# Second group's seven-product MLPs: input sums and parts spread over the first steps, weight splits at the head of a step, first two pairs interleaved

## The chip, the core and the metric

The kernel runs on one core of a Trainium2 chip. The metric is the time of one execution on the device in microseconds (us), the median of three runs. TensorE (PE) multiplies matrices, VectorE (DVE), ScalarE (ACT) and GpSimd (POOL) work element by element, and SyncE (SP) issues most of the transfers. Each engine takes its instructions strictly in the order in which they were written.

## What is computed

An attention with mixing across heads, and behind it two MLPs on the same 1792 tokens (4 batches of 448), all in float32:

```python
def _moe_ref(x, w_in, w_out):       # x (1792, 768), w_in (768, 2048), w_out (2048, 768)
    h = x @ w_in
    r = np.maximum(h, 0.0)
    g = r * r
    return g @ w_out

def _moe2_ref(x, w_in, w_out):
    h = x @ w_in
    g = h * np.clip(h + 3.0, 0.0, 6.0) / 6.0
    return g @ w_out

def reference(...):
    attn = _attn_ref(q, k, v, w_pre, w_post)        # per batch, 12 heads, 448 x 448
    x = attn.transpose(0, 2, 1, 3).reshape(B * S, H * D)
    return _moe2_ref(_moe_ref(x, ...), ...)
```

## The kernel before

The four batches are worked in two groups of two. For each group the attention runs first, then both MLPs. The order is written by hand: what stands in the program is what each engine's queue holds. The change touches only the MLPs of the second group (`SevenMlps`) and the last slots of the attention before them. Group 2 has no further attention to hide behind, so its MLPs stand alone at the end of the program.

Numbers are carried as a high part and a low part (`wh`, `wl`; `xh`, `xl`; `gh`, `gl`): ACT writes the high part as a rounded copy, DVE or POOL then writes the low part, source minus high part. A product is three matmuls, high by high, low by high, high by low.

The first matrix product of each MLP is done with seven block products in place of eight. A *pair* `j` is two blocks of 128 hidden features (`2j`, `2j+1`) for the two batches (`e` = 0, 1); the 768 input features are two halves of 3 blocks. Each product `P1` to `P7` multiplies one combination of weight blocks by one of inputs:

```python
FACTORS = {
    "P1": ("A11", "B11"), "P2": ("A12", "B21"), "P3": ("S4", "B22"), "P4": ("A22", "T4"),
    "P5": ("S1", "T1"), "P6": ("S2", "T2"), "P7": ("S3", "T3"),
}
```

A, B are blocks of weights and inputs; S1 = A21+A22, S2 = S1-A11, S3 = A11-A21, S4 = A12-S2 and T1 = B12-B11, T2 = B22-T1 (the tile `t2`), T3 = B22-B12, T4 = B21-T2 are sums made on DVE. A *step* is one product of one pair: 9 matmuls of 448 columns (3 blocks by 3). P1 and P2 share a PSUM bank (`bm`), P6, P5 and P3 another (`bo`), P7 and P4 a third (`bx`): a later product is added on top of an earlier one, so the earlier sum has to be read out of the bank before the later product may start. P1 is read by a copy on ACT (`s`), P6, P5, P7, P3 and P4 by an addition on DVE (`u`, `s`); the activation makes `g`, and `gh`/`gl` are its parts.

An MLP runs in two parts of 8 hidden blocks: 28 steps of products (4 pairs), then 8 steps of the second matrix product (`project`, 36 matmuls each, two halves of outputs `dg`). So group 2 has four stages of 28 steps, each followed by 8 projection steps. `steps` is sorted by `7 * j + SLOTS[name]`; in the first part of each MLP, P2 and P1 of the first two pairs have slots of their own.

`run` walks over the steps. At step `t` before the change:

- deferred work of earlier steps comes first (`todo[t]`, filled by `later`: the second half of the activation, then `last`, which makes `gh` on ACT and `gl` on POOL);
- then the weights for three steps ahead are split (`make`, `AHEAD = 4` buffers): `wh` on ACT, `wl` on DVE for A12, S3, S1 and on POOL for the others. With A11's split DVE also makes the three sums of the pair (L783 to L785); S4 (L790) follows when A12 and S2 have both been split;
- then come the 9 matmuls and the reading of their bank.

The inputs of the first MLP are prepared in the last slots of the attention (`opening`, `between`): the parts of B11 and B21 and the sums T1. At the head of `run`, `last_inputs` then does the rest at once: for each of 3 columns T3, `t2`, the part of T2 and T4, and then the parts of T1, T3, B22 and T4. For the second MLP, `finish` of the last projection step of the first one calls the same `last_inputs` (T1 has its parts by then).

## Time and profile before

| | us |
|---|---|
| three runs | 1478.33, 1482.08, 1482.3 |
| median | 1482.08 |
| profiled execution, its own time | 1478.12 |
| its span, first to last instruction | 1476.3 |

| engine | busy us | share of the span |
|---|---|---|
| PE | 1386.4 | 94% |
| DVE | 905.4 | 61% |
| ACT | 701.4 | 48% |
| POOL | 641.1 | 43% |

The mean granted TensorE clock is 0.985 of full speed. Group 2's MLPs run from 972.1 us to the end. A busy PE is no sign of full pace, since matmuls are pipelined and one that runs at half clock is busy too: the pace of a stage is its time divided by its matmuls. The waits that count are those that PE has, and each must be followed back through the queues of the other engines.

### The profile page before, as it was taken

Reading aid. Unit: us, or ns where it says so; the run is one execution under the profiler, and the core shown is the slowest. Engines: PE = TensorE matmul, PEld = TensorE weight load, DVE = VectorE, ACT = ScalarE, POOL = GpSimd, SP = SyncE. Lnnn points to the kernel's source line nnn. Section 1 sums busy time; section 2 is a strip of 40 time slices with the busy share of each in tenths; the row PEclk is TensorE's granted clock in tenths of the full one; section 3 lists DMA queues with packets and bytes.
Section 4 is the critical chain, followed back from the end, with each engine's and each line's share of the span. In section 5 each row is a group of like instructions: output and inputs, shape, how many; then the busy total and the mean of one; then the engine's idle time right before and its main releaser. Section 6 shows DMA issues by size and latency. Waiting matters only on the chain. (4 is left out here: it accounts for less than half of the span.)

```text
span 1476.3 us, 23273 instructions
## 1 busy us (share of the span) xinstructions
PE 1386.4 (94%) x8368; PEld 1231.7 (83%) x8368; DVE 905.4 (61%) x1662; ACT 701.4 (48%) x1428; POOL 641.1 (43%) x677
## 2 busy tenths in 40 slices
PE   8889998999999999999989999969999996999999
PEld 4778887999999999998978788857898785789788
DVE  4887566877665788775466866777307437721731
ACT  4776665555332455444366666633233324533530
POOL 1767675333200133200046767745525634552551
PEclk9999999999999999999999999979999998999999
DMA  5444533555555555666444454401211210121121
GB/s 145 117 141 113 147 102 105 177 160 161 163 158 162 159 160 161 177 199 197 164 119 130 115 142 116 133 13 44 75 44 54 65 54 21 55 65 44 43 69 70
DMA packets 72215, 167.56 MB, mean 113 GB/s; under 512 B 9125, under 2 KB 47525, under 8 KB 72101
## 3 DMA queue, kind: packets, MB, share of 16 engines
q1 hardware_dynamic: 68645, 160.59, 37.3%
q10 hardware_dynamic: 3456, 5.51, 1.0%
q8 instruction: 65, 1.06, 0.3%
q14 instruction: 49, 0.40, 0.1%
HBM read 96.86 MB, written 30.67 MB: 86 GB/s over the span
## 5 line engine op out<-in xcount | busy, mean ns | idle before, releaser
L226 POOL TENSOR_TENSOR tl<-t,th 120x448 fp32r<-120x448 f32 x165 | 193.3, 1171 | 31.8 <-ACT th L224 30.5
L281 PEld LDWEIGHTS ps_o<-w2s,p 120*112 120x112 f32 (+1 forms) x1440 | 173.2, 178 | 23.9 <-POOL w2s L270 14.2
L281 PE MATMUL ps_o<-w2s,p 120*112 120x120 f32 (+1 forms) x1440 | 180.1, 268 | 8.6 <-POOL w2s L270 8.6
L571 POOL TENSOR_TENSOR gl<-g,gh 128x448 fp32r<-128x448 f32 x40 | 52.3, 1309 | 210.7 <-ACT gh L570 164.1
L250 ACT ACTIVATE p<-ps_m,mx 120x448 f32<-120x448 f32 x180 | 113.2, 629 | 64.3 <-PE ps_o L281 29.1
L296 DVE COPY a<-ps_o 112x480 f32<-112x480 f32 (+1 forms) x176 | 114.3, 650 | 29.2 <-PE ps_o L281 28.0
L270 POOL TENSOR_SCALAR w2s<-w2f,rz 120x120 f32<-120x120 f32 x180 | 69.3, 385 | 131.0 <-DVE rz L262 119.1
L224 ACT ACTIVATE th<-t 120x448 fp32r<-120x448 f32 x180 | 102.6, 570 | 47.7 <-POOL tl L226 19.2
L242 DVE TENSOR_REDUCE mx<-ps_m 120x1 f32<-120x448 f32 x180 | 109.2, 606 | 19.5 <-PE ps_m L235 19.5
L535 ACT ACTIVATE wh<-arena 128x384 fp32r<-128x384 f32 x128 | 62.0, 516 | 115.4 <-PE bs L591 104.8
L536 DVE TENSOR_TENSOR wl<-arena,wh 128x384 fp32r<-128x384 f32 x128 | 69.1, 568 | 77.0 <-ACT wh L535 75.8
L767 POOL TENSOR_TENSOR wl<-arena,wh 128x384 fp32r<-128x384 f32 x64 | 64.9, 1032 | 102.4 <-ACT wh L766 102.4
L965 PE MATMUL ps_a<-gh,wl 128*128 128x448 f32 x272 | 99.6, 366 | 1.6 <-POOL wl L767 1.4
L181 POOL TENSOR_TENSOR ql<-qr,qh 128x440 fp32r<-128x440 f32 (+1 forms) x42 | 48.6, 1156 | 117.8 <-ACT qh L180 105.6
L965 PE MATMUL ps_a<-gh,wh 128*128 128x448 f32 x272 | 99.3, 365 | 0.0
L591 PE MATMUL ps_a<-gh,wh 128*128 128x448 f32 x256 | 93.7, 366 | 0.0
L591 PE MATMUL ps_a<-gh,wl 128*128 128x448 f32 x256 | 93.4, 365 | 0.0
L233 PE MATMUL ps_m<-th,w1h 120*120 120x448 f32 x180 | 81.6, 453 | 8.0 <-ACT p L250 6.6
L308 PE MATMUL ps_x<-a,v 112*64 112x110 f32 (+1 forms) x1536 | 84.6, 264 | 4.5 <-DVE xr L316 3.4
L766 ACT ACTIVATE wh<-arena 128x384 fp32r<-128x384 f32 x64 | 32.8, 519 | 116.7 <-PE bs L965 73.3
L308 PEld LDWEIGHTS ps_x<-a,v 112*64 112x64 f32 x1536 | 74.6, 138 | 10.3 <-DVE xr L316 3.8
L235 PE MATMUL ps_m<-tl,w1h 120*120 120x448 f32 x180 | 68.9, 383 | 12.6 <-POOL tl L226 12.6
(200 smaller groups left out, 3862.7 us busy)
## 6 DMA issues: line engine op xcount, KB each, us to landing
arena<-in_dram SPq DMA_DIRECT2D x64, 768.0 KB
t<-s SPq DMA_DIRECT2D x176, 210.0 KB
keep<-arena SPq DMA_DIRECT2D x64, 384.0 KB
arena<-keep SPq DMA_DIRECT2D x64, 384.0 KB
qr<-in_dram SPq DMA_DIRECT2D x60, 110.0 KB
v<-in_dram SPq DMA_DIRECT2D x12, 448.0 KB
outT_dram<-ot ACTq DMA_DIRECT2D x24, 224.0 KB
kr<-in_dram SPq DMA_DIRECT2D x18, 224.0 KB
```

Of the source, the lines that this page charges most:

```text
L224: nc.scalar.activation(th[:rows], tt[:rows], AF.Copy)
L226: eng.tensor_tensor(out=tl[:rows], in0=tt[:rows], in1=f(th[:rows]), op=ALU.subtract)
L233: nc.tensor.matmul(m[:rows, :S], lhsT=w1h[:rows, :rows], rhs=th[:rows], start=True, stop=False)
L242: nc.vector.reduce_max(mx[:rows], m[:rows, :S], axis=AX.X, negate=True)
L250: nc.scalar.activation(pt[:rows], m[:rows, :S], AF.Exp, bias=mx[:rows], accum_out=z[:rows])
L270: nc.gpsimd.tensor_scalar(w2s[:rows, :G * ni].rearrange("p (g i) -> p g i", g=G), w2f[:rows, :, :ni], rz[:rows], 1.0, op0=ALU.mult, op1=AL ...
L281: nc.tensor.matmul(o[:JP, q * G * ni:(q + 1) * G * ni], lhsT=pt[:rows, q * JP:(q + 1) * JP], rhs=w2s[:rows, :G * ni], start=True, stop=True)
L296: nc.vector.tensor_copy(dst, src)
L308: nc.tensor.matmul(xo[e * D:(e + 1) * D, k * n:(k + 1) * n], lhsT=self.v[:, q, g, :], rhs=self.aa[c][:, q, g, :n], start=(q == 0), stop=(q ...
L536: nc.vector.tensor_tensor(out=wl, in0=src, in1=f(wh), op=ALU.subtract)
L591: nc.tensor.matmul(acc[d, e][:, :S], lhsT=lw[q][:, wc], rhs=rw[fc, e], start=(fc == 0 and k == 0), stop=(fc == NF - 1 and k == 2))
L965: nc.tensor.matmul(acc[d, e][:, :S], lhsT=lw[:, d * P:(d + 1) * P], rhs=rw[fc, e], start=(fc == 0 and k == 0), stop=(fc == nu * UF - 1 and ...
```

## The change

- **Input sums and parts are spread.** `t2` is made as early as its inputs are there (`between`, and `finish` for the second MLP). `last_inputs` is gone: `second_parts` makes the parts of T2 and the sums T4, and `late_parts` puts the parts of T1 (first MLP alone), T3 with its sum, B22 and T4 into `todo`, one name every two steps, from step 0 on (second MLP: from its third step on).
- **Weights are split at the head of a step.** `todo` is now worked off at the end of a step, behind its own split, matmuls and bank reading (`finish_step`).
- **The sums of the weights** are made with S2's split and not with A11's.
- **The first two pairs of the first part are interleaved**: P1, P1, P2, P2, P6, P6, P5, P5, P7, P7, P3, P3, P4, P4.
- In the attention's last slots the parts of B11 and B21 come four slots earlier, the first three splits one in each of the last three slots. The loads of the weights stand at the same place of SP's queue as before.
- `g` alternates between two pairs of buffers, and the last three hidden blocks have both parts in the tile that held six low parts; it is taken when it is first needed.

The diff, cut to its core:

```diff
-                            if part == 0:
-                                at = {(0, "P2"): 1, (1, "P1"): 0.5, (1, "P2"): 3}.get((j, name), at)
+                            if part == 0 and j < 2:
+                                at = 2 * ("P1", "P2", "P6", "P5", "P7", "P3", "P4").index(name) + j
...
-            if name == "A11":
+            if name == "S2":
                 nc.vector.tensor_tensor(out=s1, in0=a21, in1=a22, op=ALU.add)
                 nc.vector.tensor_tensor(out=s2, in0=s1, in1=a11, op=ALU.subtract)
                 nc.vector.tensor_tensor(out=a21, in0=a11, in1=a21, op=ALU.subtract)
...
         def second_x(self, c):
-            self.sum_x("T3", c)
-            t2 = sh.tile([P, S], F32, tag="w0", name=f"t2{self.gi}_{c}", bufs=2)
+            t2 = self.t2[c] = sh.tile([P, S], F32, tag=("w0", "w0", "w1")[c], name=f"t2{self.gi}_{c}", bufs=2)
             nc.vector.tensor_tensor(out=t2, in0=self.source("B22", c), in1=self.source("T1", c), op=ALU.subtract)
-            self.part_x("T2", c, t2)
-            nc.vector.tensor_tensor(out=self.source("T4", c), in0=self.source("B21", c), in1=t2, op=ALU.subtract)
+        def second_parts(self):
+            for c in range(KH):
+                self.part_x("T2", c, self.t2[c])
+            for c in range(KH):
+                nc.vector.tensor_tensor(
+                    out=self.source("T4", c), in0=self.source("B21", c), in1=self.t2.pop(c), op=ALU.subtract)
+        def late_parts(self, t, names):
+            for name in names:
+                for c in range(KH):
+                    def step(name=name, c=c):
+                        if name == "T3":
+                            self.sum_x("T3", c)
+                        self.part_x(name, c)
+                    self.later(t + (c + 1) // 2, step)
+                t += 2
...
-                self.load, lambda: None, lambda: self.make(), lambda: [self.make() for _ in range(2)]]
+                lambda: None, self.load, lambda: None, lambda: None, lambda: None, self.make, self.make, self.make]
...
                 if c < KH:
                     self.sum_x("T1", c)
-        def last_inputs(self, with_t1):
-            for c in range(KH):
-                self.second_x(c)
-            for name in (("T1",) if with_t1 else ()) + ("T3", "B22", "T4"):
-                for c in range(KH):
-                    self.part_x(name, c)
+                else:
+                    self.second_x(c - KH)
...
+        def finish_step(self, t):
+            for fn in self.todo.pop(t, []):
+                fn()
...
+            self.count += 1
+            g = (sh, self.mp)[self.count % 2].tile(
+                [P, S], F32, tag=("w1", "g")[self.count % 2], name=f"g{nm}", bufs=2)
+            if (fc, e) not in self.gh:
+                self.new_hidden_last(nm)
...
                         self.part_x("T1", d)
+                    else:
+                        self.second_x(d)
             if part == 1 and which == 0 and e == 1 and dg == 1:
-                self.last_inputs(False)
+                self.second_parts()
+                self.late_parts(t + 3, ("T3", "B22", "T4"))
...
-            self.last_inputs(True)
+            self.second_parts()
+            self.late_parts(0, ("T1", "T3", "B22", "T4"))
...
             for t, (kind, which, part, j, name, n, wants) in enumerate(self.steps):
-                for fn in self.todo.pop(t, []):
-                    fn()
                 while self.made < min(used + self.AHEAD, len(self.wanted)):
                     self.make()
                 used += len(wants)
...
                     self.hidden(t, which, j, name, n)
+                    self.finish_step(t)
                     continue
...
-                        self.finish(which, part, dg, e, acc)
+                        self.finish(t, which, part, dg, e, acc)
+                self.finish_step(t)
```

In the rows below a weight tile is `wh1_<unit>_<factor>` (unit 0 is pair 0, unit 2 pair 1, unit 4 pair 2), `gh1_0_0_<block>_<batch>` the high part of a hidden block, `s11_<unit>` the copy of P1, `u21_<unit>` the reading of P6, `xh1`/`xl1` the parts of B11, B21, T1 and B22.

ACT's queue at the beginning of the first MLP of group 2, from the last part of T2 to the copy of P1 of the first pair; before:

```order
L813 ACTIVATE T2h1_0_10683<-t21_2_10706 128x448
L813 ACTIVATE xh1_0_10379<-xr1_7978 128x448 x3
L813 ACTIVATE T3h1_0_10685<-xr1_7978 128x448 x3
L813 ACTIVATE xh1_0_10379<-xr1_7978 128x448 x3
L813 ACTIVATE T4h1_0_10691<-xr1_7978 128x448 x3
L766 ACTIVATE wh1_0_S2_10736<-arena1_10545 128x384
L914 ACTIVATE s11_0_10752<-ps_P11_0_10742 128x448
```

and now:

```order
L813 ACTIVATE T2h1_0_10684<-t21_2_10660 128x448
L766 ACTIVATE wh1_2_A12_10702<-arena1_10487 128x384
L931 ACTIVATE s11_0_10716<-ps_P11_0_10706 128x448
L813 ACTIVATE xh1_0_10256<-xr1_7978 128x448
L766 ACTIVATE wh1_0_S2_10723<-arena1_10487 128x384
L931 ACTIVATE s11_2_10739<-ps_P11_2_10729 128x448
```

Twelve parts no longer stand ahead of the first copy, and a split of S2 stands ahead of the second one.

DVE's queue in the same place, the last entries up to the reading of P6 of the first pair; before:

```order
L816 TENSOR_TENSOR xl1_0_10380<-xr1_7978,xh1_0_10379 128x448 x2
L816 TENSOR_TENSOR T4l1_0_10691<-xr1_7978,T4h1_0_10691 128x448
L790 TENSOR_TENSOR arena1_10545<-arena1_10545 128x384
L767 TENSOR_TENSOR wl1_2_A12_10755<-arena1_10545,wh1_2_A12_10754 128x384
L767 TENSOR_TENSOR wl1_0_S1_10771<-arena1_10545,wh1_0_S1_10770 128x384
L880 TENSOR_TENSOR g1_0_0_0_10783<-r1_0_0_0_10784 128x448
L767 TENSOR_TENSOR wl1_0_S3_10788<-arena1_10545,wh1_0_S3_10787 128x384
L909 TENSOR_TENSOR u21_0_10801<-ps_P61_0_10791,s11_0_10752 128x448
```

and now:

```order
L790 TENSOR_TENSOR arena1_10487<-arena1_10487 128x384
L820 TENSOR_TENSOR xr1_7978<-xr1_7978 128x448
L767 TENSOR_TENSOR wl1_0_S1_10769<-arena1_10487,wh1_0_S1_10768 128x384
L820 TENSOR_TENSOR xr1_7978<-xr1_7978 128x448
L816 TENSOR_TENSOR T3l1_0_10687<-xr1_7978,T3h1_0_10686 128x448
L820 TENSOR_TENSOR xr1_7978<-xr1_7978 128x448
L897 TENSOR_TENSOR g1_0_0_0_10762<-r1_0_0_0_10763 128x448
L767 TENSOR_TENSOR wl1_2_S1_10792<-arena1_10487,wh1_2_S1_10791 128x384
L926 TENSOR_TENSOR u21_0_10805<-ps_P61_0_10795,s11_0_10716 128x448
```

The sums of T3 (L820) and one of its low parts now stand between S4's sum (L790) and the reading of P6.

ACT's queue a pair later, where it comes to the split of S2 of the third pair (unit 4); before:

```order
L766 ACTIVATE wh1_4_A11_10880<-arena1_10545 128x384
L863 ACTIVATE gh1_0_0_0_1_10668<-g1_0_0_1_10894 128x448
L766 ACTIVATE wh1_2_S3_10898<-arena1_10545 128x384
L863 ACTIVATE gh1_0_0_1_0_10670<-g1_0_1_0_10912 128x448
L766 ACTIVATE wh1_4_S2_10916<-arena1_10545 128x384
```

and now:

```order
L766 ACTIVATE wh1_4_A11_10927<-arena1_10487 128x384
L880 ACTIVATE gh1_0_0_0_1_10668<-g1_0_0_1_10923 128x448
L766 ACTIVATE wh1_4_S2_10948<-arena1_10487 128x384
L880 ACTIVATE gh1_0_0_2_1_10676<-g1_0_2_1_10941 128x448
L766 ACTIVATE wh1_4_A12_10966<-arena1_10487 128x384
```

Splits and high parts alternate in both. What differs is whose they are: before, a `gh` in front of a split is that of the step just ended, now it is that of the step before that one.

## Rows read from the trace of the kernel before

**Rows 1.** Windows by stage: length; busy us (count) by engine; clock, DMA share, GB/s

```profile
972.09:1015.84 43.75, 30.84 (x128) 26.47 (x127) 31.88 (x43) 18.19 (x38) 24.82 (x20) 0.80 0.08 28
1015.84:1046.23 30.39, 27.48 (x127) 23.20 (x126) 24.39 (x31) 12.61 (x27) 20.27 (x17) 1.00 0.18 60
...
1105.79:1163.40 57.61, 53.52 (x253) 46.72 (x252) 44.14 (x59) 24.53 (x52) 34.17 (x29) 1.00 0.16 52
1163.40:1224.06 60.66, 59.14 (x290) 53.90 (x288) 18.18 (x27) 14.03 (x27) 25.71 (x24) 1.00 0.19 56
1224.06:1265.20 41.14, 28.39 (x128) 25.01 (x126) 29.66 (x41) 19.28 (x39) 21.67 (x18) 0.83 0.09 29
1265.20:1296.62 31.42, 27.26 (x127) 23.19 (x126) 22.74 (x31) 17.12 (x34) 19.26 (x18) 1.00 0.19 63
...
1355.56:1413.75 58.19, 53.37 (x254) 46.72 (x252) 40.52 (x58) 31.15 (x62) 32.12 (x29) 1.00 0.17 55
1413.75:1472.68 58.93, 58.84 (x289) 53.73 (x287) 9.41 (x14) 9.29 (x18) 18.98 (x19) 1.00 0.17 60
```

**Rows 2.** Waits of PE, 960 to 1477 us: total, times, longest

```profile
PE ps_P L902 <- ACT s L914: 20.2, 2, 10.5
PE ps_P L902 <- POOL wl_S L767: 9.4, 13, 1.3
...
PE ps_x L308 <- DVE xr L316: 0.9, 1, 0.9
PE bs L965 <- DVE y L977: 0.8, 1, 0.8
```

**Rows 3.** Timeline of ACT, first MLP's beginning: start, us, instruction [idle before]

```profile
979.41 0.58 ACT L813 ACTIVATE T2h<-t 128x448 fp32r<-128x448 f32 x1 [2.30 <-DVE t L826]
...
985.90 0.52 ACT L914 ACTIVATE s<-ps_P 128x448 f32<-128x448 f32 x1
```

**Rows 4.** Timeline of PE at the end of that wait and behind it

```profile
986.47 0.74 PE L902 MATMUL ps_P<-xh,wh_A 128*128 128x448 f32 x1 [10.47 <-ACT s L914]
...
992.03 0.57 PE L902 MATMUL ps_P<-T2h,wh_S 128*128 128x448 f32 x1
992.40 0.57 PE L902 MATMUL ps_P<-T2h,wl_S 128*128 128x448 f32 x1
```

**Rows 5.** Timeline of DVE and POOL, first MLP's beginning

```profile
970.30 1.16 DVE L820 TENSOR_TENSOR xr<-xr 128x448 f32<-128x448 f32 x2
...
984.57 3.05 DVE L816 TENSOR_TENSOR xl<-xr,xh 128x448 fp32r<-128x448 f32 x2
...
987.10 3.01 POOL L816 TENSOR_TENSOR T4l<-xr,T4h 128x448 fp32r<-128x448 f32 x2
```

**Rows 6.** Timeline of DVE, ACT, POOL and PE ahead of a later P6

```profile
1006.41 0.62 DVE L909 TENSOR_TENSOR s<-ps_P,s 128x448 f32<-128x448 f32 x1
...
1011.31 0.58 ACT L863 ACTIVATE gh<-g 128x448 fp32r<-128x448 f32 x1 [2.53 <-DVE g L867]
1011.79 0.92 ACT L766 ACTIVATE wh_S<-arena 128x384 fp32r<-128x384 f32 x2
...
1013.06 2.29 POOL L767 TENSOR_TENSOR wl_S<-arena,wh_S 128x384 fp32r<-128x384 f32 x2
...
1014.12 0.47 PE L902 MATMUL ps_P<-T2h,wl_S 128*128 128x448 f32 x1 [1.30 <-POOL wl_S L767]
```

**Rows 7.** Groups of instructions by line, 1015.84 to 1046.23 us: busy, mean ns | idle

```profile
L864 POOL TENSOR_TENSOR gx<-g,gh 128x448 fp32r<-128x448 f32 x9 | 11.4, 1275 | 10.5 <-ACT gh L863 10.5
...
L767 POOL TENSOR_TENSOR wl_A<-arena,wh_A 128x384 fp32r<-128x384 f32 x4 | 5.4, 1347 | 0.0
...
L767 POOL TENSOR_TENSOR wl<-arena,wh 128x384 fp32r<-128x384 f32 x1 | 1.0, 1003 | 0.0
```

**Rows 8.** PE and the clock at an earlier, shorter wait

```profile
741.94 0.46 PE L195 MATMUL bs<-khl,qh 128*110 128x448 f32 x1 [2.96 <-DVE z L256]
...
742.00:746.00 4.00, 2.66 (x9) 1.94 (x10) 1.36 (x4) 2.00 (x4) 0.37 (x1) 0.61 0.33 107
```

More of the change, by code (lines that the diff above doesn't have):

```diff
@@ L737, in __init__ @@
             self.arena, self.loaded, self.freed, self.made = None, 0, set(), 0
-            self.ready, self.split_done, self.sides, self.todo = {}, set(), 0, {}
-            self.x = {}
+            self.ready, self.split_done, self.sides, self.todo, self.t2 = {}, set(), 0, {}, {}
+            self.x, self.count = {}, 0
         def wr(self, n):
@@ L844, in between @@
                     self.sum_x("T1", c)
-        def last_inputs(self, with_t1):
-            for c in range(KH):
-                self.second_x(c)
-            for name in (("T1",) if with_t1 else ()) + ("T3", "B22", "T4"):
-                for c in range(KH):
-                    self.part_x(name, c)
+                else:
+                    self.second_x(c - KH)
         def later(self, t, fn):
             self.todo.setdefault(t, []).append(fn)
+        def finish_step(self, t):
+            for fn in self.todo.pop(t, []):
+                fn()
         def act(self, t, which, fc, e, h, psum):
             nm = f"{self.gi}_{which}_{fc}_{e}"
-            g = sh.tile([P, S], F32, tag="w1", name=f"g{nm}", bufs=2)
+            self.count += 1
[3 more added lines that the diff above has]
+                self.new_hidden_last(nm)
             gh, gl = self.gh[fc, e], self.gl[fc, e]
@@ L939, in new_hidden @@
                     for p, of in (("h", self.gh), ("l", self.gl)):
-                        if p == "l" and fc >= nf - KC:
+                        if fc >= nf - KH:
                             continue
@@ L951, in some, with new_hidden_last @@
                     of[fc, e] = mp.tile([P, S], F32R, tag=f"g{p}{fc}_{e}", name=f"g{p}{nm}_{fc}_{e}")
-                if not rest and k > KC:
-                    gx = sh.tile([P, KC, T], F32R, tag="xr", name=f"gx{nm}")
-                    for fc in range(nf - KC, nf):
-                        for e in range(NB):
-                            self.gl[fc, e] = gx[:, fc - nf + KC, e * S:(e + 1) * S]
-            return some
+            return some
+        def new_hidden_last(self, nm):
+            gx = sh.tile([P, KC, T], F32R, tag="xr", name=f"gx{nm}")
+            nf = NF // self.PARTS
+            for k in range(KH):
+                for e in range(NB):
+                    cols = slice(e * S, (e + 1) * S)
+                    self.gh[nf - KH + k, e], self.gl[nf - KH + k, e] = gx[:, k, cols], gx[:, KH + k, cols]
         def project(self, u, e, parts, acc, nu):
@@ L967, in project, with finish @@
                             start=(fc == 0 and k == 0), stop=(fc == nu * UF - 1 and k == 2))
-        def finish(self, which, part, dg, e, acc):
+        def finish(self, t, which, part, dg, e, acc):
             cols, end = slice(e * S, (e + 1) * S), which == 1 and dg == DG - 1 and e == NB - 1
@@ L989, in finish @@
                         self.part_x("T1", d)
+                    else:
+                        self.second_x(d)
             if part == 1 and which == 0 and e == 1 and dg == 1:
-                self.last_inputs(False)
+                self.second_parts()
+                self.late_parts(t + 3, ("T3", "B22", "T4"))
         def run(self, mp, behind):
-            nu = NU // self.PARTS
+            self.mp, nu = mp, NU // self.PARTS
             some = self.new_hidden(mp, 0, 0)
```

## The prediction

> **What bounds the kernel now.** I first asked the windows by stage, since the change touches only the stretch from 972 us on, in which TensorE is never off the path. In [rows 1] each line is a stage of group 2's MLPs: a stage of 28 steps is 252 matmuls (9 a step; the counts also catch a neighbour or two), cut in two halves of 126 in the first part of each MLP; a projection stage is 288. The reader is to divide: the last line, 288 matmuls in 58.93 us, runs at 0.2046 us a matmul and hardly waits, which makes a floor. At that pace 126 matmuls take 25.8 us and 252 take 51.6. Over the floor are, in the order of the lines: 18.0 (first half, first MLP), 4.6, 6.0, 1.7 (a projection), 15.3 (first half, second MLP), 5.6, 6.6, 0. Sum 57.8 us. That is all the change can win there.
>
> Then I asked who lets PE wait. [Rows 2]: two long waits for the copy `s` of P1, 20.2 us together, and many short ones for low parts of weights. The first long one is read from ACT's queue. T2's last high part begins at 979.41, the copy of P1 only at 985.90 [rows 3]; by the order shown with the change, twelve parts stand between, although P1 had long been computed. PE starts again at 986.47 after 10.47 us [rows 4]. Behind it matmuls come 0.37 apart (992.03 to 992.40) and not 0.20: the granted clock is at 1.2 GHz, 0.80 over that stage and 0.83 in the second MLP's [rows 1].
>
> The short waits are read in [rows 6]. DVE reads P3's bank at 1006.41 and makes `g`; ACT makes `gh` and splits a weight; DVE makes that weight's low part and only then reads P4's bank and makes its `g`; `gh` follows on ACT at 1011.31 after 2.53 idle, the split of S2 behind it at 1011.79, POOL's low part at 1013.06, and P6 goes on at 1014.12 after 1.30 of waiting. No engine is full there; each waits in its queue for another.
>
> **The change, part by part.** The sum is made against the profiled execution's own 1478.1 us, 4.0 under the median of the three runs (1482.08), which contains another of 1478.33.
>
> *Attention's end.* The weight sums leave DVE's queue ahead of the reading of the last values, for which PE waited 0.9 [rows 2]. Gain 0.9. The moved parts of B11 and B21 and the first splits are as many as before, on engines with gaps; SP's queue has the same order. I cost these at nothing.
>
> *First MLP's beginning.* Durations: two DVE operations of 448 columns in a row take 1.16 [rows 5], 0.55 to 0.6 each, an ACT one 0.5 to 0.6 [rows 3]. While POOL works, neither runs freely: two on DVE take 3.05 us, two on POOL 3.01 in the same time [rows 5], 1.5 for one of each. So a DVE operation waits out the POOL operation that it meets; one that reads PSUM does not (0.62 at 1006.41 [rows 6], as elsewhere). With this I wrote out the new queues by hand. Let P1 start at 971.2.
> - P1 of both pairs ends at 974.9. `t2` and T2's parts: T2's last high part ends at 974.4, a split and the copy `s` follow, 975.4. PE waits 0.6.
> - The second copy now stands behind S2's split, and that behind DVE: T2's middle low part, three sums T4, A12's low part, T1's low part, two weight sums, eight operations of 0.55 and one met by POOL (0.9): 973.8 to 979.2. Split and copy 980.2; P2 of pair 0 ended at 977.3. PE waits 3.0.
> - S2 of pair 1 comes through DVE, ACT and POOL once more, 985.1, with PE there at 984.2: 0.9.
> - P5 may start when DVE has read P6's bank. In the order shown seven operations stand ahead of that reading behind S4's sum (985.6), four of them behind ACT, which itself needs DVE: T3's sum, a split, its low part, T3's next part, and so on: 0.55 or so each plus the hand-offs and two met by POOL, 992.7, reading 993.3. P6 ended at 986.8. PE waits 6.6: **the long wait does not go, it moves to P5**, at two thirds of its length.
> - P5 of pair 1 likewise: 1.5.
>
> Sum 12.6. Without any meeting with POOL the same queues give 8.7; with every operation met, about 18, as long as now. I take 12.6, since the rows show most pairs met. Clock: a wait of 2.96 us was already followed by 0.61 of full clock [rows 8], so 6.6 will be too. In the stage now, some 24 matmuls of 0.37 cost 24 x 0.17 = 4.1; I put 1.5 to the new one, since at the slow pace the wait of P5's second pair vanishes (bounds 0 and 4). 14.1 against 18.0: gain 3.9.
>
> *Second MLP's beginning.* Same queues, but T1 has its parts already and pair 0 and 1's P1 come out of the projection. The waits are 2.7 (A12's low part behind the T4 sums), 1.0, 0.2, 5.9 (P5) and 0.4: 10.2, with the clock 11.7. Now 15.3: gain 3.6 (from 0 to 8).
>
> *Steady steps.* The split for step t+3 is now written ahead of step t's reading, and ahead of it stands the `gh` of step t-2, not t-1 (third pair of fences). Its buffer is free when step t starts, its `gh` is over by then, and three steps of 9 x 0.2046 = 1.84 us remain, 5.5 us, for 0.5 on ACT, 1.0 to 1.35 on POOL [rows 7] and what POOL has queued. So the chain of [rows 6] is cut. What is late next: in the first MLP S2's three sums come on DVE behind P4's reading, its `g` and P2's `g`; S2's low part is on time by a few tenths, but POOL then has two low parts of `g` (1.28 in the mean of [rows 7]) ahead of S4's, which ends 1.0 to 1.4 after P3 wants it. I take 1.2 a pair: 2.4 left in the second half-stage, 3.6 in the next. In the second MLP `g` comes a step later, S4's low part stands ahead of the last `gl`, and I find no wait; 0.5 left in each. Gains 4.6 - 2.4 = 2.2, 6.0 - 3.6 = 2.4, 5.6 - 0.5 = 5.1, 6.6 - 0.5 = 6.1. In the projection of [rows 1] with 1.7 over, the 0.8 for `y` [rows 2] stays: gain 0.9.
>
> Deferred work that comes a step later delays `gh` and `gl`, but the projection that reads the last of them comes to those blocks in its fourth step, 3 x 36 x 0.2046 = 22 us on: nothing. The extra buffers of `g` take no time. The tile for the last blocks waits for the last reader of the inputs, T4's parts, some 10 us before it is needed: nothing.
>
> Sum: 0.9 + 3.9 + 3.6 + 2.2 + 2.4 + 5.1 + 6.1 + 0.9 = 25.1. 1478.1 - 25.1 = 1453.0. The runs shown lie between that execution and 4 us more; I stay at **1453**.
>
> **The rivals.**
> - *The port between DVE and POOL is the bound.* One pair, 7 steps, needs in the first MLP 4 weights' low parts of 1.0 on POOL [rows 7], 4 of `g` of 1.17 (an estimate, 1.0 x 448 / 384 columns), and on DVE 11 operations that meet them, each worth the 1.35 - 1.0 = 0.35 by which POOL's grow when met [rows 7]: 8.7 + 3.8 = 12.5 us, against 7 x 1.84 = 12.9 on PE. That speaks for it: without its waits PE would leave the port full. Against it: the second MLP has one operation fewer that meets, and three steps of slack. If it decides, the first MLP's steady stages keep what they have, the second's win 2 to 3 each, the beginnings 1 each: gain 10, 1468. The Trainium skill, "SBUF — State Buffer", section "Who interferes with whom", has an exclusive lock in which the second to issue fully blocks; by that rule too the two add up, as the 1.5 us for one of each shows.
> - *The clock.* The change turns one long wait into four or five in a row, each of which can bring TensorE down to 1.2 GHz, as the 2.96 us did [rows 8]. If both half-stages ran at 0.37 throughout, each would take 126 x 0.37 = 46.6 us, with waits hidden beside it, against 43.75 and 41.14 [rows 1]: 8.4 us lost instead of 7.5 won, 1469. Against it: now, 126 matmuls behind a longer wait saw 24 slow ones. The Trainium skill, "TensorE: Matmul & The Clock Gate", section "HAM oscillation — how this bites in real kernels", says that such gaps pay the penalty again each time.
> - *The waits vanish nearly all*: 8.7 and some 7 at the beginnings, the clock up, nothing over 0.3 in the steady stages: gain 42, 1436.
> - *Slower*: POOL's queue in steady steps. S4's low part now stands behind two of `gl`, and a DVE operation may come in between each. If it ends more than 2.3 us after P3 wants it (what a pair of the first MLP waits now, 4.6 / 2), every pair loses; at 3.5 in the 12 pairs behind the beginnings it is 12 x 1.2 = 14 lost, nothing won at the beginnings: 1492. My working has 1.4 at worst.
> - *It does not do what it says*: the split finds its buffer still in use and the short waits stay; only the beginnings win, 8: 1470. The order of queues speaks against it.
>
> **How the numbers follow.** Forecast (waits moved to P5, most of the short ones gone) 1453: 0.55, on its own 1445 to 1462. Port 0.12, clock 0.08, vanish 0.15, slower 0.04, not doing what it says 0.06. The range reaches half into "vanish" and up to the port and clock cases: 1438 to 1470. 0.3% is 4.4 us, about what can be told from no change with this kernel: all but the slower case and the tails of the port and clock cases are faster by more. Faster 0.90, same 0.05, slower 0.05.
>
> **What would show it.** After: no wait for `s` over 4 us; the longest wait of PE is P5's first matmul, released by DVE's reading of P6, 4 to 8 us, in both MLPs; first half-stages of 38 to 42 us; second MLP's 28-step stage at 52 to 53 and the first's at 54 to 56; clock under 1 only around P5. Wrong if the waits for POOL's `wl_S` in the steady steps keep 5 us or more in the second MLP, if P5 does not wait, or if the clock is down over most of a half-stage.

## The result and the profile after

The median of the changed kernel is 1467.65 us (1465.66 to 1470.23, four runs), that of the kernel before in the same session 1481.89 (1478.33 to 1482.3): a ratio of 0.991, 95% interval 0.9886 to 0.9934. It is faster by 14 us, about 1%. The forecast was 1453, a gain of 25 against the profiled run and 29 against the median: the sign held, the time lies in the range, and half of the gain did not come. The profiled run took 1469.05 us. One disturbed execution, of 4755.51 us in run e6 below, is left out of the medians and ratios.

The stages after, in the columns of [rows 1]:

```profile
976.75:1016.35 39.60, 30.02 (x128) 26.11 (x127) 33.94 (x45) 17.69 (x36) 24.51 (x20) 0.87 0.12 40
1016.35:1046.72 30.37, 27.02 (x127) 23.26 (x126) 27.33 (x33) 13.61 (x29) 20.64 (x17) 1.00 0.17 53
...
1106.11:1163.70 57.59, 53.08 (x253) 46.91 (x252) 43.42 (x59) 24.71 (x52) 32.92 (x28) 1.00 0.17 55
1163.70:1224.09 60.39, 59.20 (x290) 53.85 (x289) 14.16 (x23) 13.93 (x27) 26.00 (x25) 1.00 0.17 53
1224.09:1261.59 37.50, 29.03 (x127) 25.23 (x126) 29.05 (x45) 18.26 (x36) 21.05 (x17) 0.91 0.13 42
1261.59:1290.58 28.99, 26.14 (x127) 23.46 (x126) 23.59 (x33) 18.26 (x36) 19.75 (x18) 1.00 0.18 55
...
1349.43:1403.78 54.35, 52.73 (x254) 46.85 (x253) 39.99 (x58) 30.57 (x62) 30.93 (x28) 1.00 0.18 59
1403.78:1463.61 59.83, 58.91 (x289) 53.81 (x287) 9.91 (x14) 9.25 (x18) 19.82 (x19) 1.00 0.17 59
```

Read the second number of each line beside [rows 1]. The first half-stages fell from 43.75 to 39.60 and from 41.14 to 37.50, as forecast (14.1 and 11.7 us over the floor were predicted, 13.8 and 11.7 came). The second half-stage and the 28-step stage of the first MLP did not move at all: 30.39 to 30.37, 57.61 to 57.59. Those of the second MLP fell by 2.4 and 3.8 where 5.1 and 6.1 were forecast.

PE's waits after, 960 to 1477 us, beside [rows 2]:

```profile
PE ps_P L919 <- ACT xh L813: 12.5, 2, 6.7
PE ps_P L919 <- ACT s L931: 6.0, 5, 2.6
PE ps_P L919 <- POOL wl_S L767: 5.6, 7, 1.4
PE ps_P L919 <- DVE u L926: 2.7, 2, 1.5
PE ps_a L985 <- POOL wl L767: 1.9, 3, 0.9
PE ps_P L919 <- ACT gx L880: 1.8, 3, 1.2
```

The two waits for `s`, 20.2 us, are gone; in their place stand two waits of P5's first matmul. The view names `xh` on ACT for them, but the timeline shows DVE's reading of P6's bank as the last to come:

```profile
998.99 0.61 DVE L926 TENSOR_TENSOR u<-ps_P,s 128x448 f32<-128x448 f32 x1
...
999.74 0.71 PE L919 MATMUL ps_P<-xh,wh_S 128*128 128x448 f32 x1 [6.67 <-ACT xh L813]
1000.25 0.57 PE L919 MATMUL ps_P<-xh,wl_S 128*128 128x448 f32 x1
1000.62 0.57 PE L919 MATMUL ps_P<-xl,wh_S 128*128 128x448 f32 x1
```

and short windows the clock (third column from the end):

```profile
999.00:1002.00 3.00, 2.26 (x6) 2.07 (x7) 3.00 (x5) 1.13 (x3) 2.57 (x2) 0.50 0.00 0
1002.00:1005.00 3.00, 3.00 (x12) 2.43 (x12) 3.00 (x5) 2.91 (x6) 2.26 (x2) 0.71 0.00 0
1005.00:1009.00 4.00, 4.00 (x21) 3.70 (x20) 3.96 (x6) 1.05 (x2) 4.00 (x4) 1.00 0.00 0
```

The reading ends at 999.60 and PE goes on at 999.74. The clock is at 1.2 GHz (0.50) behind the 6.67 us of idle, matmuls come 0.37 apart, and it is back at full speed by 1005.

The steady steps of the first MLP, DVE and POOL over the last third of one pair:

```profile
1140.68 1.15 POOL L881 TENSOR_TENSOR gl<-g,gh 128x448 fp32r<-128x448 f32 x1 [1.17 <-ACT gh L880]
1141.05 1.19 DVE L767 TENSOR_TENSOR wl_S<-arena,wh_S 128x384 fp32r<-128x384 f32 x1 [1.06 <-ACT wh_S L766]
1142.16 0.61 DVE L926 TENSOR_TENSOR u<-ps_P,u 128x448 f32<-128x448 f32 x1
...
1145.08 0.55 DVE L785 TENSOR_TENSOR arena<-arena 128x384 f32<-128x384 f32 x1
...
1145.88 1.01 POOL L767 TENSOR_TENSOR wl_S<-arena,wh_S 128x384 fp32r<-128x384 f32 x1 [4.05 <-ACT wh_S L766]
1146.84 2.27 POOL L881 TENSOR_TENSOR gl<-g,gh 128x448 fp32r<-128x448 f32 x2
1149.06 1.31 POOL L767 TENSOR_TENSOR wl_S<-arena,wh_S 128x384 fp32r<-128x384 f32 x1
```

This is the order that the prediction described: S2's low part (1145.88) behind the sums, then two low parts of `g`, then S4's low part, for which P3 waits. The prediction gave it 1.2 us a pair and had S2's low part on time; PE waits 0.9 for S2's and 1.55 for S4's, 2.4 a pair. One could now blame the late sums. The experiments say otherwise.

### The profile page after: what moved, and what is told of

Its sections match the earlier page's. It is cut to its first block, busy times and chain, and to the rows that moved or that the text cites. A ratio compares the mean times of both kernels' runs of the same rounds, so it can differ in the third digit from the quotient of the medians.

```text
span 1467.3 us, 23244 instructions
## 1 busy us (share of the span) xinstructions
PE 1387.9 (95%) x8368; PEld 1234.7 (84%) x8368; DVE 902.9 (62%) x1662; ACT 701.2 (48%) x1428; POOL 639.9 (44%) x677
## 5 line engine op out<-in xcount | busy, mean ns | idle before, releaser
L767 POOL TENSOR_TENSOR wl<-arena,wh 128x384 fp32r<-128x384 f32 x64 | 65.6, 1044 | 100.9 <-ACT wh L766 100.9
L591 PE MATMUL ps_a<-gh,wh 128*128 128x448 f32 x256 | 93.7, 366 | 0.0
L591 PE MATMUL ps_a<-gh,wl 128*128 128x448 f32 x256 | 93.3, 365 | 0.0
L579 PE MATMUL ps_h<-xl,wh 128*128 128x448 f32 x192 | 70.6, 368 | 0.0
L579 PE MATMUL ps_h<-xh,wh 128*128 128x448 f32 x192 | 70.5, 367 | 0.0
```

Of the source, the lines that this page charges most:

```text
L579: nc.tensor.matmul(hp[:, :S], lhsT=lw[c // KH][:, c % KH * P:(c % KH + 1) * P], rhs=rw[:, c, cols], start=(k == 0), stop=(k == 3 * KC - 1))
L591: nc.tensor.matmul(acc[d, e][:, :S], lhsT=lw[q][:, wc], rhs=rw[fc, e], start=(fc == 0 and k == 0), stop=(fc == NF - 1 and k == 2))
```

## The experiments

For every run: microseconds over the floor (0.2046 a matmul, as in the prediction) in the six stages of the first products, worked out from the windows of each trace, from first matmul to first matmul. The column `all` adds the four projection stages. Then comes the time: the median for before, after, e1, e2, e6, e7, e12, e13, e14 and e17, one execution for the others. The runs were made in several sessions, in which the medians of the kernel before were 1478.8 to 1481.9, so a ratio is always to the kernel before of the same session.

| kernel | 1st MLP: first half | second half | 28 steps | 2nd MLP: first half | second half | 28 steps | all | time |
|---|---|---|---|---|---|---|---|---|
| before | 18.0 | 4.6 | 6.1 | 15.4 | 5.6 | 6.6 | 58.7 | 1481.89 |
| after | 13.8 | 4.6 | 6.0 | 11.7 | 3.2 | 2.8 | 44.9 | 1467.65 |
| e1 sums early | 13.8 | 7.7 | 6.6 | 11.7 | 8.0 | 1.8 | 52.2 | 1473.36 |
| e2 split last | 15.2 | 9.3 | 5.9 | 13.1 | 6.8 | 7.8 | 60.5 | 1481.51 |
| e4 no gl | 14.7 | -0.2 | -0.2 | 12.0 | 0.0 | -0.3 | 25.0 | 1446.32 |
| e5 late T3 | 15.1 | 2.3 | 6.1 | 8.6 | 5.7 | 2.8 | 43.2 | 1464.27 |
| e6 Square on ACT | 13.8 | 0.5 | 1.0 | 10.9 | 3.2 | 2.8 | 35.7 | 1458.32 |
| e7 half of gl on DVE | 14.3 | 2.9 | 3.3 | 11.6 | 2.7 | 2.9 | 37.5 | 1458.68 |
| e8 pad, PSUM | 14.4 | 5.1 | 6.8 | 11.9 | 4.0 | 3.9 | 47.4 | 1467.73 |
| e9 pad, SBUF | 14.0 | 10.1 | 10.0 | 10.8 | 9.5 | 7.2 | 65.6 | 1488.97 |
| e10 pairs apart | 15.1 | 3.9 | 6.0 | 13.0 | 3.5 | 2.8 | 48.1 | 1465.9 |
| e11 parts at once | 16.6 | 3.9 | 6.0 | 14.0 | 3.2 | 2.8 | 49.2 | 1472.43 |
| e12 Square and gl | 13.9 | 0.3 | 0.8 | 12.2 | 2.7 | 3.3 | 33.0 | 1454.93 |
| e13 all | 11.5 | 0.4 | -0.1 | 8.6 | 4.3 | 0.4 | 25.0 | 1447.15 |
| e14 gl after weights | 13.9 | 3.9 | 5.6 | 11.2 | 3.7 | 3.6 | 45.8 | 1468.63 |
| e15 and sums early | 14.4 | 4.6 | 4.7 | 11.5 | 3.6 | 1.3 | 44.3 | 1467.15 |
| e16 pad, same place | 15.9 | 7.3 | 9.1 | 11.0 | 5.9 | 5.0 | 58.5 | 1478.81 |
| e17 all, gl after | 11.6 | 0.9 | -0.1 | 8.7 | 7.8 | 1.0 | 29.8 | 1450.76 |

Single times of one kernel differ by up to 5 us; the stages decide. A stage that an edit leaves alone repeats within 0.1 us: the first MLP's 28 steps are at 6.0 or 6.1 in after, e5, e10 and e11, the second MLP's at 2.8 in all four.

Part of some entries is the clock and no waiting. In the first MLP's 28 steps the mean granted clock is 1.00 in before, after, e6, e7, e8 and e15, but 0.97 in e1, e14 and e16 and 0.94 in e9; in the second MLP's it is 0.97 in e2 and e9. There some matmuls follow longer waits 0.37 us apart, which adds up to 1.5 us in e1, 1.2 in e14, 1.6 in e16 and 2.6 in e9, and in the second MLP's stage to 1.5 in e2 and in e9.

### The order of the sums, and the order in a step

**e1.** All but the first two pairs:

```diff
-            if name == "S2":
+            if name == ("A11" if self.units[n][2] >= 4 else "S2"):
```

> Edit: the three sums of a pair's weights go back to the split of A11 (two steps earlier than S2's), for every pair but the first two of a first part. Theory A (the sums at S2's split are late: TensorE waits for S2's low part, and POOL, held by it, reaches S4's low part only behind two low parts of g): the waits of P6 and P3 for POOL's weight parts, 0.9 and 1.4 to 1.55 us a pair in the trace of after, go. The first MLP's 28-step stage falls from 6.0 us over the floor to 0.5 to 2.5, its second half-stage from 4.6 to 2 to 3, the second MLP's 28-step stage from 2.8 to 0.5 to 1.5; 5 to 8 us in all, 1460 to 1463. Rival B (DVE and POOL together are full through their shared port): moving the sums in time changes nothing, the 28-step stage stays at 5.5 to 6.5 and the time at 1466 to 1469. Rival C (it is only the order on POOL, two low parts of g ahead of S4's weights): P6's wait goes, P3's stays, the stage falls by 2 to 4 us to 2.5 to 4, time 1463 to 1465.

The first MLP's 28 steps:

```profile
1106.64:1164.82 58.18, 53.89 (x253) 48.20 (x252) 45.03 (x59) 24.87 (x52) 33.91 (x29) 0.97 0.16 55
```

P6's wait went and P3's grew from 1.55 to 2.18 us: the pair still takes 15 us, the first MLP's stage is at 6.6, and both second half-stages lose 3 to 5 us. Without the 1.5 us of slow matmuls the stage is at 5.1, so the early sums win 0.9 there at most, where 3.5 to 5.5 were expected: the theory of the late sums falls for the first MLP. In the second it holds for 1.0 us.

**e2.** `finish_step(t)` stands at the head of a step, ahead of the splits, again.

> Edit: only the order inside a step is undone: a step begins with the work left by earlier steps (g, its high and low part, x's parts) and then splits its weights, as in the kernel before; the rest of the change stays. Theory A (late sums cost the steady part, and the new order neither helps nor hurts much): steady stages within 1.5 us of after, the sums' waits stay, time 1464 to 1472. Rival C (the new order is itself what puts S4's part late or, the other way, what saves the second MLP's 28-step stage, 6.6 to 2.8): the second MLP's stage goes back to 5 to 6.6 us over the floor, time 1470 to 1476.

The time is that of the kernel before (ratio 1.0009, 0.9998 to 1.002), slower than both expectations, with the interleaving and the spreading kept. The beginnings keep 2.8 and 2.3 us of gain, but the second half-stages (9.3 and 6.8) and the second MLP's 28 steps (7.8) are worse than before the change. So without the new order in a step nothing of the whole gain is left. The first MLP's 28-step stage, at 5.9, does not answer to this order.

### Is it the resource that DVE and POOL share?

The shared resource is here what the rival "the port" named: something that a POOL instruction and a DVE instruction without an input in PSUM cannot have at the same time. Such a DVE instruction has its inputs in SBUF, where all tiles lie that are not PSUM banks.

**e4.** POOL's `gl` is left out and the product with it takes `gh` again, so that the low part of the hidden layer is missing; this kernel is a probe alone:

```diff
-                nc.gpsimd.tensor_tensor(out=gl, in0=g, in1=f(gh), op=ALU.subtract)
-  ... (wh, self.gh), (wl, self.gh), (wh, self.gl)
+  ... (wh, self.gh), (wl, self.gh), (wh, self.gh)
```

> Edit: POOL makes no low part of g in this group's MLPs (the third product takes the high part again, so the low part of the hidden layer is left out); four POOL instructions of 1.0 to 1.35 us a pair go, a third of what DVE and POOL do together. Rival B (the shared port is the bound): the 28-step stage of the first MLP falls from 6.0 us over the floor to under 1. Theory A (late sums): S2's low part still comes late, P6's wait of 0.9 to 1.2 us a pair stays, P3's goes: 3 to 5 us over the floor.

All four steady stages fall to the floor. The groups of the first MLP's 28-step stage, of after and then of e4, show what POOL's work had done to DVE's:

```profile
L767 DVE TENSOR_TENSOR wl_S<-arena,wh_S 128x384 fp32r<-128x384 f32 x8 | 7.7, 957 | 3.7 <-ACT wh_S L766 3.7
L926 DVE TENSOR_TENSOR u<-ps_P,s 128x448 f32<-128x448 f32 x8 | 4.9, 618 | 2.2 <-PE ps_P L919 2.2
```

```profile
L767 DVE TENSOR_TENSOR wl_S<-arena,wh_S 128x384 fp32r<-128x384 f32 x8 | 4.5, 556 | 3.8 <-ACT wh_S L766 3.8
L925 DVE TENSOR_TENSOR u<-ps_P,s 128x448 f32<-128x448 f32 x8 | 4.9, 617 | 2.2 <-PE ps_P L918 2.2
```

The low part with two SBUF inputs takes 957 ns beside `gl` and 556 without it; the reading with one input in PSUM takes 618 and 617. The Trainium skill, "SBUF — State Buffer", section "Who interferes with whom", says the same: a DVE instruction with two SBUF inputs contends with a GpSimd instruction that reads SBUF, and one with at most one SBUF input, outside the two-port modes, does not. The trace agrees in both.

**e6** and **e7** take work off that resource, **e8** and **e9** add some.

```diff
-            if which == 0 and not psum:
-                nc.vector.scalar_tensor_tensor(out=g, in0=h, scalar=0.0, in1=h, op0=ALU.max, op1=ALU.mult)
...
-                    nc.vector.tensor_tensor(out=g, in0=r, in1=r, op=ALU.mult)
+                    nc.scalar.activation(g, r, AF.Square)
```

> Edit: in the first MLP ScalarE makes g (Relu, then Square, two operations) for all blocks, where VectorE made it; a pair loses four DVE operations of 0.63 us that read and write SBUF, POOL's queue and its order stay. Port theory (in after one pair keeps the resource that DVE's SBUF operations and POOL share busy for 12.8 us of the 12.9 that TensorE needs, and what it idles between two hand-offs, 2.3 us, is what TensorE waits): demand falls to 10.3 us a pair, the first MLP's 28-step stage falls from 6.0 us over the floor to 0 to 2.5, its second half-stage from 4.6 to 1 to 3; the second MLP as in after. Time 1459 to 1464. POOL's queue alone (its order, its eight operations a pair): those waits stay, 1466 to 1469. If ScalarE becomes late (it gets 7 operations of some 0.55 us a pair more): waits for gh's weights on ACT, 1470 or more.

```diff
+                eng = nc.vector if odd else nc.gpsimd
-                nc.gpsimd.tensor_tensor(out=gl, in0=g, in1=f(gh), op=ALU.subtract)
+                eng.tensor_tensor(out=gl, in0=g, in1=f(gh), op=ALU.subtract)
```

> Edit: every second low part of g is made by DVE instead of POOL, in both MLPs: two POOL operations of 1.15 us a pair become two DVE ones of some 0.6. Port theory: the shared resource's demand falls by 2 x 0.55 = 1.1 us a pair, the 28-step stages fall from 6.0 and 2.8 to 2 to 4 and 0.5 to 2 us over the floor, 1460 to 1464. POOL's queue alone is the bound: a still larger fall, POOL loses 2.3 us a pair, both stages under 1.5, 1457 to 1461. DVE's queue alone is the bound: slower, 1469 or more.

The first MLP's 28 steps of e6 and then of e7:

```profile
1101.28:1153.84 52.56, 51.95 (x254) 47.01 (x252) 29.69 (x44) 35.13 (x74) 28.99 (x27) 1.00 0.18 58
```

```profile
1102.15:1157.00 54.85, 52.54 (x253) 46.92 (x252) 42.91 (x66) 24.72 (x52) 26.99 (x23) 1.00 0.18 58
```

e6: the first MLP's stage falls from 6.0 to 1.0 with POOL's instructions kept (ratio to before 0.9849, 0.9818 to 0.9879). Their order is not quite kept: `gh` and `gl` come a step later, so that one `gl` and not two stands between S2's low part and S4's. e7: 3.3, so that more instructions on DVE made the kernel faster (0.986, 0.984 to 0.9881); the forecast fall in the second MLP's stage did not come, and three of the four projections won 0.8 to 1.2 each instead.

> Edit: DVE makes each of the two readings of P6's and P5's banks twice, so two more DVE operations of 0.62 us a pair that read PSUM. Port theory (an operation that reads PSUM does not take the shared resource): little in the 28-step stages, 0 to 2 us more in each than in after. DVE's queue is the bound: 1.2 us a pair, 3 to 5 us more in each 28-step stage. Both: the half-stages grow by what P5's first matmul waits more, 0.6 each.

> Edit: DVE makes g of P7's and P3's blocks twice, so two more DVE operations of some 0.63 us a pair that read and write SBUF only, in the places behind the readings of PSUM. Port theory: 1.3 us a pair and more where they meet POOL's, 3 to 6 us more in each 28-step stage than in after, clearly more than the run with two more readings of PSUM. DVE's queue is the bound: the same as that run within 1 us a stage.

e8 makes `add` twice for P6 and P5, e9 makes `g` of P7 and P3 twice. The 28-step stages of e8 (first two lines) and e9:

```profile
1102.50:1160.88 58.38, 53.10 (x253) 46.93 (x252) 48.71 (x67) 24.98 (x53) 33.30 (x29) 1.00 0.16 55
1346.80:1402.29 55.49, 52.92 (x253) 46.68 (x252) 45.08 (x66) 30.78 (x62) 30.95 (x28) 1.00 0.17 57
```

```profile
1109.89:1171.41 61.52, 55.91 (x254) 49.38 (x252) 47.53 (x65) 24.02 (x51) 32.87 (x28) 0.94 0.16 52
1364.26:1423.03 58.77, 54.88 (x253) 48.08 (x252) 44.92 (x65) 30.36 (x61) 30.89 (x28) 0.97 0.16 54
```

DVE is busier in e8 (48.71 against 47.53), and yet the stages grew by 0.8 and 1.1 there and by 3.9 and 4.4 in e9, where 2.6 and 1.5 are slow matmuls. DVE's queue is not the bound. One doubt was left. In the rows of after each piece of a pair waits for the one before it, from one pair to the next: P4's reading, `g`, sums, S2, two `gl`, S4, P3. The reliefs e4, e6 and e7 also shorten this loop, and the two pads stood in different places.

**e14, e15, e16.** e14 keeps all work and moves `gl` behind the next step's splits; e15 makes the sums early in the 28-step stages too; e16 puts an SBUF operation where e8 has its PSUM one.

```diff
-                nc.gpsimd.tensor_tensor(out=gl, in0=g, in1=f(gh), op=ALU.subtract)
+                self.lows.append(lambda: nc.gpsimd.tensor_tensor(out=gl, in0=g, in1=f(gh), op=ALU.subtract))
...
                     self.make()
+                while self.lows:
+                    self.lows.pop(0)()
```

> Edit: POOL's low parts of g are issued behind the next step's weight splits, so that S4's low part stands ahead of the two low parts of g; nothing is taken away. Loop theory: in after S4's low part ended at 1150.37, behind two low parts of g of 2.27 together, and the loop took 15.8 us against 12.9; without the two it is 13.6 to 14, so the first MLP's 28-step stage falls from 6.0 us over the floor to 2 to 3, its second half-stage from 4.6 to 2.5 to 3.5; 1461 to 1464. Shared resource full (13.1 us a pair before any gap): the low parts of g only come later and the gaps stay, 5 to 6.5 over the floor, 1466 to 1469.

> Edit: as the run before it, and the three sums at A11's split in the 28-step stages. Loop theory: the loop loses the sums (1.65 us) too and is shorter than 12.9, both 28-step stages 0 to 1 us over the floor. Shared resource full: 5 to 6.5 in the first MLP's as in after, the second MLP's 1 to 2.

```diff
                 add(kv[j, 2], kv[j, 1])
+                nc.vector.tensor_tensor(out=kv[j, 2], in0=kv[j, 2], in1=kv[j, 2], op=ALU.max)
...
                 add(kv[j, 3], kv[j, 1])
+                nc.vector.tensor_tensor(out=kv[j, 3], in0=kv[j, 3], in1=kv[j, 3], op=ALU.max)
```

> Edit: behind the readings of P6's and P5's banks DVE runs one more operation on the values just read (the maximum of a tile with itself), with SBUF operands, two of some 0.6 us a pair in the very place where the pad with PSUM operands stood (6.8 and 3.9 us over the floor in the 28-step stages, 0.8 and 1.1 more than after). Shared resource: it costs 2 to 4 us more than after in each 28-step stage. A matter of place alone (the loop): the same as the PSUM pad within 0.7.

The 28-step stages of e14, of e15 and of e16:

```profile
1105.64:1162.80 57.16, 54.16 (x253) 48.30 (x252) 42.24 (x59) 24.70 (x52) 33.02 (x28) 0.97 0.18 56
1349.34:1404.45 55.11, 52.96 (x253) 46.77 (x252) 40.72 (x58) 30.57 (x62) 31.48 (x28) 1.00 0.17 58
```

```profile
1106.45:1162.72 56.27, 53.03 (x253) 46.75 (x252) 44.60 (x59) 24.65 (x52) 33.80 (x27) 1.00 0.17 56
1350.07:1402.96 52.89, 52.30 (x254) 46.92 (x252) 41.88 (x58) 30.59 (x62) 32.65 (x28) 1.00 0.19 60
```

```profile
1107.15:1167.76 60.61, 54.40 (x253) 48.24 (x252) 49.66 (x67) 25.21 (x53) 35.53 (x28) 0.97 0.16 53
1356.67:1413.23 56.56, 53.19 (x254) 46.59 (x253) 46.62 (x66) 30.68 (x62) 32.39 (x28) 1.00 0.18 56
```

With the two `gl` out of the loop the first MLP's stage falls by 0.4 us, or 1.6 without the 1.2 us of slow matmuls in e14. With the sums out as well, at full clock, it falls by 1.3. The loop theory had 3 to 4 and 5 to 6: the loop is worth about a quarter of the 6.0 at most and is not the cause of the rest. In the same place an SBUF operation costs 3.0 and 2.2 us a stage, a PSUM one 0.8 and 1.1. Of the 3.0, 1.6 are slow matmuls in e16. The three steady stages in which e16 and e8 both had the full clock tell the two apart without that: in the two second half-stages and the second MLP's 28 steps the SBUF operation costs 2.7, 2.7 and 2.2 us, the PSUM one 0.5, 0.8 and 1.1.

**What the resource holds.** From the trace I took the time in which POOL or a DVE instruction without a PSUM input runs, once each moment:

| first MLP's 28 steps | stage | shared resource busy | idle |
|---|---|---|---|
| before | 57.6 | 47.9 | 9.7 |
| after | 57.6 | 47.5 | 10.1 |
| e1 | 58.2 | 47.0 | 11.2 |
| e2 | 57.5 | 47.4 | 10.1 |
| e14 | 57.2 | 46.9 | 10.3 |
| e15 | 56.3 | 45.4 | 10.9 |
| e7 | 54.9 | 44.8 | 10.0 |
| e8 | 58.4 | 48.1 | 10.3 |
| e16 | 60.6 | 50.5 | 10.1 |
| e9 | 61.5 | 51.2 | 10.3 |
| e6 | 52.6 | 39.9 | 12.7 |
| e13 | 51.5 | 38.3 | 13.2 |

In the ten kernels that wait there, the stage is the resource's work plus 9.7 to 11.2 us that no order filled; in the last two PE's own 51.6 sets the time. One pair of after (1130.34 to 1145.58) has it busy for 13.1 of 15.2 us; PE needs 12.9. Seven steps at a time, the stage of after takes 12.8, 14.0, 15.8 and 15.0 us with the resource busy for 9.5, 11.1, 13.4 and 13.6: the first seven run at PE's pace, with 3.4 of the 10.1 idle us in them, and most of the waiting lies where the work is over PE's 12.9. In the second MLP's stage it is 44.9 of 54.35 after, 45.5 of 58.2 before: less work than in the first MLP, in after under 12.9 in each seven steps, and there the order did matter (6.6 to 2.8, and 1.3 with e15). Why the rest of the idle part is there is not settled.

### The beginnings

**e5.** T3's, B22's and T4's parts two steps later (`if name == "T3": t += 2` in `late_parts`).

> Edit: x's parts T3, B22 and T4 start two steps later in both MLPs, so that DVE reads P6's results before it makes T3's sums. Theory A, for the longest wait (P5's first matmul, 6.7 and 5.9 us, waits for a PSUM bank that DVE reads only after its part of the spread-out x sums): each falls by 2 to 5 us, the two first half-stages from 39.6 to 35 to 38 and from 37.5 to 33 to 36. Rival (P5's wait is not DVE's queue but ACT's, which makes the high parts in the same steps, or the wait only moves to P7 or P3, whose inputs are now later): the half-stages stay within 1 us.

P5's waits fall to 1.0 and 0.5 us, but others grow: the first MLP's half-stages trade 1.2 against 2.3, the second's 3.1 against 2.4, 1.7 in all.

**e10** has the old order of the first two pairs, **e11** calls `step()` at once in `late_parts` instead of `self.later`.

> Edit: the order of the first two pairs' steps is the kernel before's again (pair 0's steps mostly ahead of pair 1's); the rest of the change stays. If the interleaving carries the gain of the beginnings: P2, P6 and P5 of pair 0 come up to two steps earlier while their inputs come no earlier, the first half-stages grow from 39.6 and 37.5 us by 2 to 4 each. If the spreading of x's parts carries it alone: both stay within 1 us. The 28-step stages stay as in after either way (57.6 and 54.4).

> Edit: T1's, T3's, B22's and T4's parts are issued in one piece ahead of the first step again and not over the first steps; the rest of the change stays. If the spreading carries the gain of the beginnings: the copy s of P1 stands behind twelve parts on ACT once more, PE waits 8 to 11 us for it in the first MLP and the half-stages come back to 42 to 45 and 40 to 43 us. If it only moves the wait (the parts take the same time on DVE, POOL and ACT wherever they stand): the wait for s comes, P5's of 6.8 and 6.0 goes, and the half-stages stay within 1.5 us of 39.6 and 37.5.

The interleaving is worth 1.3 us in each first half-stage, less than expected. Without the spreading PE waits 11.5 us for `s` again, and P5's wait is gone: the spreading exchanged the one for the other and won 2.8 and 2.2.

```profile
PE ps_P L919 <- ACT s L931: 23.5, 4, 11.5
```

### Versions

> Edit: both reliefs of the shared resource together, g of the first MLP on ScalarE (Square) and every second low part of g on DVE. Port theory: the first MLP's demand falls from 12.8 to some 9.2 us a pair, its 28-step stage to 0 to 1 us over the floor, the second's stays near 2.8 to 2.9 since its waits outlived the single relief, the projections lose the 0.9 they win with DVE's share of gl; 1455 to 1459. If ScalarE is the next to be late, 1459 to 1463.

> Edit: as the run with both reliefs, and T3's, B22's and T4's parts two steps later, and the three sums at A11's split in the second parts alone, whose stages begin with weights in store. Port theory with freed room: late parts no longer hurt what follows them, the second half-stages keep 0 to 3 us over the floor and the first lose 0 to 3, the second MLP's 28-step stage falls from 2.8 to 0.5 to 1.5; 1450 to 1456. If the beginnings are bound by the same fixed demand, T3's delay only moves the wait, and the whole is 1455 to 1458.

> Edit: as the run with all reliefs (1447.15), and the low parts of g, on both engines, behind the next step's weight splits. With room on the shared resource the stages that run at the floor can win nothing (28-step stages 0 to 0.4 over it); what is left is in the two beginnings and the second MLP's second half-stage (11.5, 8.6 and 4.3 over the floor). If POOL's order counts there: 1 to 3 us less, 1444 to 1446; if not, 1446 to 1449.

e12 is e6 and e7 (ratio 0.9841, 0.9824 to 0.9859). e13 is e12, e5 and the sums at A11 in the second parts: 1447.15 us, ratio 0.9785 (0.977 to 0.9799), by the two ratios some 18 us faster than the changed kernel. Its 28-step stages:

```profile
1096.27:1147.77 51.50, 51.50 (x253) 47.23 (x252) 31.69 (x51) 37.69 (x78) 25.08 (x24) 1.00 0.19 62
1330.57:1382.48 51.91, 51.70 (x253) 47.15 (x252) 42.35 (x65) 30.73 (x61) 26.34 (x23) 1.00 0.19 61
```

With room on the resource the later T3 pays: the first MLP's half-stages together are 2.3 under e12's, the second's 1.9. e17, with e14's order on top, was 3.6 us slower than e13, against both expectations; its trace has it in the second MLP's second half-stage (7.8 against 4.3, with a granted clock of 0.95). That half-stage's remainder was not looked into further.

## Why the prediction was wrong by half

- *The base.* The 25.1 us were taken from the profiled execution's 1478.1, and the forecast stayed at 1453 although the median was 3.8 us higher: of the 14.65 us between 1453 and 1467.65 that is 3.8.
- *Attention's end, 0.9.* Right: the wait of 0.9 for `xr` went, and from the wait of 0.6 for `a`, which is in both traces, P1 is 6.1 us away before (965.97 to 972.09) and 5.0 after (971.75 to 976.75). P1 starts at 976.75 and not 972.09, because this execution was 5 us late from 104 us on, where both kernels are the same.
- *The first MLP's beginning, 3.9, and the second's, 3.6.* Right: 4.2 and 3.6, with the waits where the queues written by hand had them (0.4, 2.8, none, 6.8 and then 0.3, for 0.6, 3.0, 0.9, 6.6 and 1.5). "The long wait does not go, it moves to P5" is in the rows above.
- *The first MLP's steady steps, 2.2 and 2.4.* Wrong, both 0. The order in the queues was right and the cause was not: the waits were put down to a chain through the queues ("No engine is full there; each waits in its queue for another", [rows 6]), and cutting the chain was counted as gain. The shared resource left no room (47.5 us of work in 57.6, over PE's pace where the waits are), and cutting the chain only moved the wait.
- *The second MLP's, 5.1 and 6.1.* Half right: 2.4 and 3.8. "I find no wait" was wrong; up to 1.5 us of the 2.8 left are the sums and `gl` ahead of S4 (e1, e15).
- *The projections, 0.9.* Wrong: the one with 1.7 over came to 1.5, and the last one lost 0.9 in a wait for POOL's low part of a weight (`ps_a`, longest 0.9, in PE's waits above).
- *The rival "the port is the bound"*, given 0.12 and 1468, describes what happened in the steady steps: the first MLP's keep what they have, the second's win 2.4 and 3.8, where it had 2 to 3. For the beginnings it had 1 each, and 4.2 and 3.6 came. That its 1468 lies so near to 1467.65 is luck, since its 10 us were taken from 1478.1 and the medians differ by 14.
- *The step that failed* is the gain for the steady steps, 2.2 + 2.4 + 5.1 + 6.1 = 15.8 us, of which 6.2 came, and behind it the weighing of that rival: it had 12.5 us of demand a pair against PE's 12.9, and the forecast took the 0.4 as room. The trace has 13.1 and some 2 idle in one pair, so 15.2. The forecast read as a full resource only one at 100%.
- *The clock* fell to 0.50 behind P5 in both MLPs, as forecast, but in the first one also behind the wait of 2.65 us for `s` (0.50 from 988 to 990 us); the half-stages' 0.87 and 0.91 are above the 0.80 and 0.83 of [rows 1].

## What to carry to other kernels

Add the work of two engines that block each other before calling neither of them full, and compare the sum with the bound engine's period with a margin for hand-offs: here a pair with 13.1 us of work needed 15.2. If that sum is near the period, reordering mostly moves waits, and moving work elsewhere (here to ScalarE, or to the faster of the two engines) removes them. A pad of equal length, once with and once without the shared operand and in the same place, tells in two runs which it is; compare stages that ran at the same granted clock.

## What was not expected of the hardware

Moving every second `gl` to DVE made DVE's own busy time in the first MLP's 28 steps fall, 43.42 to 42.91 us, though DVE ran 7 instructions more. In e7's groups a `gl` on DVE takes 626 ns, and the low part of S, 957 in after, 795:

```profile
L767 DVE TENSOR_TENSOR wl_S<-arena,wh_S 128x384 fp32r<-128x384 f32 x8 | 6.4, 795 | 1.6 <-ACT wh_S L766 1.6
...
L883 DVE TENSOR_TENSOR gl<-g,gh 128x448 fp32r<-128x448 f32 x6 | 3.8, 626 | 4.5 <-ACT gh L881 4.5
```

And executions differ by 4 to 5 us before the changed part is reached, where the code is the same. Windows of before and of after, at the same code, clock third from the end:

```profile
60.00:100.00 40.00, 36.65 (x325) 32.15 (x325) 30.18 (x73) 28.47 (x63) 28.19 (x34) 1.00 0.45 126
```

```profile
60.00:100.00 40.00, 36.19 (x290) 31.46 (x290) 28.36 (x70) 27.16 (x58) 25.68 (x31) 0.91 0.44 126
```

The run with 0.91 did less of the attention's work in that time (290 matmuls against 325). What starts it was not tried.
